# Zeros of the experts' results on ScalarE in place of GpSimd, a conversion moved, ten more constant products

## The chip, the cores and the metric

The kernel runs on one core of one Trainium2 chip. TensorE multiplies matrices into PSUM; VectorE, ScalarE and GpSimd work element by element; SP issues most transfers. The metric is device time in microseconds, the median of the runs.

## What is computed

The reference is clustered attention, a gated mixture of experts on its result, and a dense two-layer block behind that:

```python
mask = q_assign[:, :, :, None] == k_assign[:, :, None, :]       # nearest of 16 centroids
scores = np.where(mask, scale * np.matmul(q, k.transpose(0, 1, 3, 2)), -1e9)
attn = np.matmul(softmax(scores), v)                             # 2 x 8 heads, 768 x 64
x = attn.transpose(0, 2, 1, 3).reshape(1536, 512)
expert_idx = np.argmax(x @ w_gate, axis=1)                       # 8 experts
for e in range(E):                                               # each token by its expert
    out[mask_e] = gate_w[mask_e, None] * (np.maximum(xe @ w1[e], 0.0) @ w2[e])
h = out @ w_in                                                   # 512 -> 2048
return (np.maximum(h, 0.0) + alpha * np.minimum(h, 0.0)) @ w_out
```

## The kernel before

The instructions of each engine run in the order in which the program gives them; there is no scheduler, so that order is the one in which they stand in the code. Engines wait for each other by semaphores.

**Opening and attention.** Eight pairs of heads are worked on in turn. For the first pair the opening (from L658 on) assigns keys and queries to centroids in two halves: `sim_pair` (L345, products with the centroids), `simev_pair` (L352, ScalarE), `simturn_pair` (L358, transposes), `simmax_pair` and `simeq_pair` (L363, L369, VectorE), `eqt_pair` (L377), `eqev_pair` (L382, ScalarE), `first_pair` (L391 and L392 on TensorE, then L396 on ScalarE and L397 on VectorE). In between stand `qhi_pair` (L310) and `qlo_pair` (L314), which split queries in two parts, and copies on SP's queue. `warm(n, ps)` (L269 to L271) puts n products of constants in TensorE's queue, whose results nobody reads; they stand at places of the opening where TensorE waits for another engine. Then the loop over query tiles begins: `scores` (L429, L430), `rowmax` (L436, VectorE), `softmax` (L446, ScalarE), transposes (L460), and products with the values (L469).

**Experts.** Tokens are sorted by expert into DRAM (`Xs`, scatters by GpSimd at L612), and the experts run in order of their token counts, `blk` 0 to 7, each with eight groups: g = 8 * blk + f. At g, `l1` makes eight (for most experts) matmuls (L1004) into one of two PSUM banks, which ScalarE empties with a Relu (L1006); `l2` makes eight matmuls (L1025) for the group of g - 2. Expert 1 (`HB`) is computed in split parts: its weights are split by `wsplit` (L984 ScalarE, L985 VectorE) from g = 7 on, its matmuls are L989 to L991. Its tokens are transposed (`x_transp`, L963) at g = 5 and g = 6 in two halves, through two PSUM banks that ScalarE (L967) and VectorE (L968) empty. At the end of an expert `y_evac` (L1034, L1036) writes its result to the columns of `x2a` and `x2b` that belong to its tokens; the columns of overflowing tokens are not written there and must be zero. So `x2a` and `x2b`, 128 x 2 x 1842 floats each, are zeroed first: eight GpSimd memsets (L943) of 921 columns, which stand right before the experts. Their memory is that of rows and offsets that the last scatters read, and so is free only when these have landed.

**Conversions.** Among the experts stand 26 conversions of the dense block's weights from 64-bit to 32-bit floats (`CONV`, L1182: how many steps at which g). One `conv_step(k)` issues `conv_bits` (L178 to L181, four VectorE instructions) for k, the store of k - 1 on SP's queue (L234), `conv_abs` (L174, ScalarE) for k + 1, and for k of 6 and more the load of k + 3 on SP's queue. For k of 2 and more, up to 4, the next conversion's target is memory that this conversion reads, so its L174 waits for this one's L181. Four more, prefetched ones have L174 at g = 2, 4, 33, 37 and their four VectorE steps one group later, ahead of that group's `x_transp`. Weight blocks of the experts (1 MB each) are loaded on SP's queue as blocks come free (L147).

In a group the order of issue is: `l1`, `l2`, `y_evac`, the small sums of g (`side`), prefetched and split steps (`ahead`), transfers, `x_transp`, then the steps of `CONV`.

Of the kernel before, what the change touches and what calls it, by code (L numbers as in the profile page):

```python
# [14 lines left out]
AF = mybir.ActivationFunctionType  # L15
# [6 lines left out]
P = 128  # L22
# [16 lines left out]
XCOLS = N + CMAX  # L39
# [52 lines left out]
def tile_cluster_attention_moe(ctx: ExitStack, tc: tile.TileContext, qk, kk, v, cen, cenr, gate, mw, m2w,  # L92
                               alpha, consts, table, pos, zeros, nowhere, out):
    nc = tc.nc
# [11 lines left out]
    cst = const.tile([P, C_END], F32, name="cst")  # L106
# [156 lines left out]
    psS = [PS[:, 1024 * i:1024 * i + S] for i in range(2)]  # L263
# [5 lines left out]
    def warm(n, ps):  # L269
        for _ in range(n):  # L270
            nc.tensor.matmul(ps[:, 0:512], oneb, oneb.unsqueeze(1).broadcast_to([P, 4, P]), start=True, stop=True)  # L271
# [36 lines left out]
    def qhi_pair(p, hh, cs=slice(0, S)):  # L308
        st, R = sets[p % 2], Rt[p]
        nc.scalar.activation(st["QB"][0:64, hh, cs], R[0:64, hh, cs], AF.Copy, scale=0.125)  # L310
# [37 lines left out]
    def simev_pair(p, hh=None):  # L348
        pr = p % NPAIR
        rs, _, ps = alone(p, hh)  # L350
        sT = once("sT", p, [P, CH], tag="fr")
        nc.scalar.activation(sT[rs], ps[rs, :CH], AF.Copy, scale=cn[rs, 3, pr:pr + 1])  # L352
# [7 lines left out]
    def simmax_pair(p, hh=None):  # L360
        _, gs, ps = alone(p, hh)
        m = once("am", p, [P, 3, 8])
        nc.vector.tensor_reduce(m[:, :, gs], groups(ps[:, :CH])[:, :, gs], AX.X, ALU.max)  # L363

    def simeq_pair(p, hh=None):
        _, gs, ps = alone(p, hh)
        n = gs.stop - gs.start
        oh = once("ohc", p, [P, CH], BF16)
        nc.vector.tensor_tensor(groups(oh)[:, :, gs], groups(ps[:, :CH])[:, :, gs],  # L369
                                pre["am"][1][:, :, gs].unsqueeze(3).broadcast_to([P, 3, n, NC]), ALU.is_equal)  # L370
# [8 lines left out]
    def eqev_pair(p, hh=None):  # L379
        rs, _, ps = alone(p, hh)  # L380
        pb = ps.bitcast(BF16)
        nc.scalar.activation(once("eT", p, [P, CH], BF16)[rs], pb[rs, :CH], AF.Copy)  # L382

    def first_pair(p, hh=None):
        rs, _, ps = alone(p, hh)
        eT = pre["eT"][1]
        if hh is not None:

            st, r0 = sets[p % 2], rs.start
            pk = (psT, psM)[hh]  # L390
            nc.tensor.matmul(pk[r0:r0 + 48, :CH], firstb[rs, r0 + NC:r0 + NC + 48], eT[rs], start=True, stop=True)  # L391
            nc.tensor.matmul(ps[rs, :CH], firstb[rs, rs], eT[rs], start=True, stop=True)  # L392
            for c in range(2):
                cs = slice(c * CH, (c + 1) * CH)
                r1 = r0 + 32 * c
                nc.scalar.activation(st["QB"][64:80, hh, cs], ps[r1:r1 + 16, :CH], AF.Relu)  # L396
                nc.vector.tensor_scalar(st["KB"][64:80, hh, cs], pk[r1:r1 + 16, :CH], 0.0, -NEG, ALU.is_le, ALU.mult)  # L397
            return
        nc.tensor.matmul(psM[:, :CH], firstb, eT, start=True, stop=True)
# [82 lines left out]
    class Route:  # L482
# [101 lines left out]
        def sum(self):  # L584
            for k in range(self.n):
                nc.vector.tensor_add(ohsum, ohsum, OH[:, self.t0 + k, :])
                yield
# [67 lines left out]
    nc.vector.tensor_scalar_add(cn[:, 2, :], cn[:, 1, :], 1e-6)  # L655
    nc.vector.reciprocal(cn[:, 3, :], cn[:, 2, :])

    warm(8, psS[1])  # L658
    qhi_pair(0, 0)
    sim_pair(0, 0)  # L660
    simev_pair(0, 0)
    warm(2, psS[1])
    qhi_pair(0, 1)
    qlo_pair(0, 0)
    copyq_pair(0, h0)
# [1 line left out]
    nc.vector.tensor_copy(firstb, cst[:, C_FIRST:C_FIRST + P])  # L667
    simturn_pair(0, 0)
    simmax_pair(0, 0)
    warm(1, psS[1])  # L670
    simeq_pair(0, 0)
    ksplit_pair(0, nc.vector, 0)
    copy_pair(0, h0)
    load_r(1)
    eqt_pair(0, 0)
    eqev_pair(0, 0)
    warm(1, psS[1])
    first_pair(0, 0)
    qlo_pair(0, 1)
    sim_pair(0, 1)  # L680
# [193 lines left out]
    def parts(blk):  # L874
        return PARTS[blk], CAPS[blk] // PARTS[blk]
# [61 lines left out]
    x2p = pool(ctx, "x2p", side="right")  # L937
    x2a = x2p.tile([P, 2, XCOLS], F32, name="x2a")
    x2b = x2p.tile([P, 2, XCOLS], F32, name="x2b")
    for t in (x2a, x2b):  # L940
        for h in range(2):
            for c in range(0, XCOLS, XCOLS // 2):
                nc.gpsimd.memset(t[:, h, c:c + XCOLS // 2], 0.0)  # L943

    def x_transp(blk, half=None):
        nt, np_ = parts(blk)
        nb = nt * np_
        xr = xrt[blk]
        if half != 1:
            xts[blk] = xtp.tile([P, 4, CMAX], F32R if blk == HB else F32, name=f"x_{blk}", tag="x")[:, :, 0:nb]  # L950
            if blk == HB:
                split["x"] = xq.tile([P, 4 * CH], F32R, name="xlo", tag="x0")[:, 0:4 * nb].rearrange("p (d n) -> p d n", d=4)
                hlo = xq.tile([P, 4 * CH], F32R, name="hlo", tag="x1")
                split["h"] = [hlo[:, CMAX * i:CMAX * i + nb] for i in range(4)]
        x = xts[blk]
        dn = 2 if 2 * nb <= 512 else 1
        for g in range(4 // dn) if half is None else range(2 * half, 2 * half + 2):
            ps = bank(2 + g % 2)[:, 0:dn * nb]
            for k in range(dn):
                d = dn * g + k  # L960
                for t in range(nt):
                    c0 = k * nb + t * np_
                    nc.tensor.transpose(ps[:, c0:c0 + np_], xr[0:np_, t, d * P:(d + 1) * P], idf[0:np_, 0:np_])  # L963
            pv = ps.rearrange("p (d n) -> p d n", d=dn)
            if blk == HB:
                cs = slice(dn * g, dn * (g + 1))
                nc.scalar.activation(x[:, cs, :], pv, AF.Copy)  # L967
                nc.vector.tensor_sub(split["x"][:, cs, :], pv, x[:, cs, :].bitcast(F32))  # L968
            elif g % 2 == 0:
                nc.scalar.activation(x[:, dn * g:dn * (g + 1), :], pv, AF.Copy)  # L970
            else:
                nc.vector.tensor_copy(x[:, dn * g:dn * (g + 1), :], pv)
# [40 lines left out]
    def l2(blk, f):  # L1013
        nb = CAPS[blk]
        ci = 4 * blk + 2 * (f // 4) + 1
        w = wslots[ci].rearrange("p (f d) -> p f d", f=4)
        h = hts.pop((blk, f))
        if f == 0:
            yps[blk] = [bank(4 + o) for o in range(4)]
        for o in range(4):  # L1020
            y = yps[blk][o][:, 0:nb]
            if blk == HB:
                thrice(y, split[1, f], o, h, split["h"][f % 4], f == 0, f == 7)
            else:
                nc.tensor.matmul(y, w[:, f % 4, o * P:(o + 1) * P], h, start=f == 0, stop=f == 7)  # L1025
        if f % 4 == 3:
            wload()
# [134 lines left out]
    def s_half(r, n):  # L1162
# [10 lines left out]
        else:  # L1173
# [5 lines left out]
    NG = 8 * NB  # L1179


    CONV = {1: 1, 2: 1, 4: 1, 10: 1, 13: 1, 17: 1, 18: 1, 19: 1, 20: 1, 21: 1, 22: 1, 24: 1, 25: 1, 27: 1, 28: 1, 30: 1,  # L1182
            32: 1, 34: 1, 36: 1, 38: 1, 40: 1, 43: 1, 45: 1, 49: 1, 52: 1, 57: 1}
    assert sum(CONV.values()) == NCA
    xt = stmp.rearrange("p a d f -> p (a d f)")[:, 0:2 * CH].rearrange("p (a c) -> p a c", a=2)
# [86 lines left out]
    for g in range(NG + LAG):  # L1272
        if g < NG:
            blk, f = divmod(g, 8)
            l1(blk, f)
        if g >= LAG:
            b2, f2 = divmod(g - LAG, 8)
            l2(b2, f2)
            if f2 == 7 and b2 + 1 < NB:
                y_evac(b2, col[b2])  # L1280

        for f_ in side.get(g, []):
            f_()
        if g == 42:
            SHL = xsp.tile([P, 2, 7, 2, P], F32R, name="SHL", tag="SHL")
        for f_ in ahead.get(g, []):
            f_()
        if g == 40:
            more = nc.values_load(ovi[0:1, 0, 2:3], min_val=0, max_val=NSEL)
        if g < NG:  # L1290
            if f == 1 and blk + 1 < NB:
                wreg[blk + 1] = reg(wi[0:1, blk + 1:blk + 2], [ET.SP], 4 * (E - 1))
                row = reg(rowi[0:1, blk + 1:blk + 2], [ET.Activation if blk else ET.SP], E * N - N)
                x_load(blk + 1, Xs[ds(row, CAPS[blk + 1]), :])
            if f == 2:
                if blk >= 1:
                    src = offi[0:1, blk:blk + 1]
                    col[blk] = ds(reg(src, COMP, N), CAPS[blk])
                    put_places(blk, ds(reg(src, [ET.SP], N), CAPS[blk]))
                else:  # L1300
                    nc.sync.dma_start(PG[col[0], :], Xs[0:CAP, DM:XW])
            if f >= 5 and blk + 1 < NB and 2 * CAPS[blk + 1] > 512:
                if f < 7:
                    x_transp(blk + 1, f - 5)
            elif f == 6 and blk + 1 < NB:
                x_transp(blk + 1)
        if g == 0:
            conv_begin(0)
        for _ in range(CONV.get(g, 0)):
            conv_step(nconv[0])  # L1310
            nconv[0] += 1
# [186 lines left out]
    with tc.For_i(0, more, 1):  # L1498
# [27 lines left out]
        h = xo.tile([P, 2 * DM], F32, name="oh")  # L1526
# [16 lines left out]
        z = bank(5)  # L1543
# [78 lines left out]
```

## Time and profile before

| | us |
|---|---|
| median of three runs | 702.34 |
| lowest, highest | 701.82, 703.73 |
| the profiled execution | 704.18 |
| its span | 702.3 |
| TensorE matmul busy in it | 679.4 (97%) |
| VectorE busy | 482.2 (69%) |
| ScalarE busy | 370.8 (53%) |
| GpSimd busy | 68.8 (10%) |

The page gives the busy time of each engine, the chain of work that ended last and the costliest groups; the trace behind it gives single instructions with start and length, and the idle time of the engine before them with what ended it. PE is TensorE's matmuls, PEld its weight loads, DVE VectorE, ACT ScalarE, POOL GpSimd. The granted clock is a share of 2.4 GHz: 0.50 is 1.2 GHz. A row with x8 merges eight instructions in a row of one kind; its length runs from the first start to the last end.

### The profile page before, as it was taken

How to read it: one execution, taken by the hardware profiler on the slowest of the kernel's cores; microseconds unless marked ns; L12 is line 12 of the kernel's file. 1: busy time of each engine (PE TensorE's matmuls, PEld its weight loads, DVE VectorE, ACT ScalarE, POOL GpSimd, SP SyncE). 2: the span in 40 equal slices, each digit the busy share in tenths (PEclk: the TensorE clock that was granted, in tenths of full speed). 3: DMA queues.
4: the chain of work that ended last, by engine and by line, in shares of the span. 5: the costliest groups of instructions: out<-in, count | busy, mean ns of one | idle time of the engine just before them, and what ended most of it. 6: DMA issues, size and time to landing. Idle time of an engine off the chain costs nothing.

```text
span 702.3 us, 11396 instructions
## 1 busy us (share of the span) xinstructions
PE 679.4 (97%) x4126; PEld 574.4 (82%) x4126; DVE 482.2 (69%) x885; ACT 370.8 (53%) x735; POOL 68.8 (10%) x75
## 2 busy tenths in 40 slices
PE   7899999999999999799999999999999999999994
PEld 3667667666677689799999999989898998898983
DVE  6877777688886569587647654687788774544552
ACT  4877778767586512433323433664556654433441
POOL 3210202203120034000000000000000020000003
PEclk8999999999999999999999999999999999999997
DMA  8345887625246045386999989554433665554412
GB/s 261 107 159 157 272 297 257 204 79 169 76 103 217 27 151 196 98 279 149 396 337 314 353 311 297 147 201 154 157 135 136 203 199 170 162 157 143 149 32 92
DMA packets 49146, 131.78 MB, mean 188 GB/s; under 512 B 8399, under 2 KB 14054, under 8 KB 44896
## 3 DMA queue, kind: packets, MB, share of 16 engines
q1 hardware_dynamic: 44424, 115.85, 50.2%
q0 software_dynamic: 3216, 12.60, 5.3%
q10 hardware_dynamic: 1447, 2.58, 1.5%
q8 instruction: 34, 0.56, 0.3%
q14 instruction: 25, 0.20, 0.1%
HBM read 98.15 MB, written 30.24 MB: 183 GB/s over the span
## 4 chain that ended last, share of the span: by engine, by line
PE 86%; DVE 6%; issue 2%; DMA 2%; ACT 2%; POOL 1%; POOLq 0%; DVEq 0%; ACTq 0%; SPq 0%
PE PS L1226 16%; PE PS L1004 10%; PE PS L1025 10%; PE PS L460 8%; PE PS L469 8%; PE PS L1360 6%; PE PS L1359 6%; PE PS L1358 6%; PE PS L429 4%; PE PS L430 4%; DVE sm L436 2%; PE PS L989 1%; PE PS L990 1%; PE PS L991 1%; PE PS L345 1%
## 5 line engine op out<-in xcount | busy, mean ns | idle before, releaser
L446 ACT ACTIVATE P<-PS,sm 128x768 f32<-128x768 f32 x96 | 86.5, 901 | 32.0 <-DVE sm L436 32.0
L436 DVE TENSOR_REDUCE sm<-PS 128x1 f32<-128x768 f32 x96 | 91.9, 957 | 15.6 <-PE PS L430 15.2
L460 PEld LDWEIGHTS PS<-cst,P 128*128 128x128 f32 x576 | 63.4, 140 | 29.5 <-ACT P L446 17.3
L460 PE MATMUL PS<-cst,P 128*128 128x128 f32 x576 | 82.4, 278 | 3.2 <-ACT P L446 1.5
L1004 PE MATMUL PS<-x,w 128*128 128x208 f32 (+6 forms) x448 | 80.2, 323 | 0.0
L1025 PE MATMUL PS<-h,w 128*128 128x208 f32 (+6 forms) x448 | 79.7, 321 | 0.0
L463 DVE COPY PT<-PS 128x384 f32<-128x384 f32 x96 | 53.0, 552 | 37.9 <-PE PS L460 37.8
L1360 PE MATMUL PS<-BH,gc 128*128 128x512 f32 x192 | 75.8, 395 | 0.0
L1359 PE MATMUL PS<-BL,gc 128*128 128x512 f32 x192 | 75.5, 393 | 0.0
L1358 PE MATMUL PS<-BH,gc 128*128 128x512 f32 x192 | 75.1, 391 | 0.0
L429 PE MATMUL PS<-KA,QA 128*128 128x512 f32 x192 | 74.1, 386 | 0.0
L1004 PEld LDWEIGHTS PS<-x,w 128*128 128x128 f32 x448 | 72.3, 191 | 0.5 <-ACT h L1006 0.3
L1025 PEld LDWEIGHTS PS<-h,w 128*128 128x128 f32 x448 | 72.7, 191 | 0.1
L469 PE MATMUL PS<-PT,V 128*64 128x384 f32 (+1 forms) x432 | 72.4, 462 | 0.0
L1226 PE MATMUL PS<-xT,SHL 128*128 128x384 f32 x336 | 68.2, 338 | 0.2 <-DVE gc L1456 0.2
L1226 PEld LDWEIGHTS PS<-xT,SHL 128*128 128x128 f32 x336 | 59.6, 188 | 4.9 <-DVE gc L1456 0.7
L462 ACT ACTIVATE PT<-PS 128x384 f32<-128x384 f32 x96 | 46.7, 486 | 28.5 <-PE PS L460 26.9
L430 PE MATMUL PS<-KB,QB 96*128 96x512 f32 x192 | 61.4, 341 | 0.0
L1006 ACT ACTIVATE h<-PS 128x208 f32<-128x208 f32 (+7 forms) x64 | 21.3, 334 | 63.7 <-PE PS L1004 55.0
L1371 POOL DMA_INDIRECT out_dram<-row,PGR x12 | 11.7, 972 | 410.0 <-ACT row L1368 400.5
L1226 PE MATMUL PS<-xB,SHL 128*128 128x384 f32 x240 | 48.5, 337 | 0.0
L1226 PEld LDWEIGHTS PS<-xB,SHL 128*128 128x128 f32 x240 | 42.9, 188 | 3.1
(270 smaller groups left out, 1124.2 us busy)
## 6 DMA issues: line engine op xcount, KB each, us to landing
w<-in_mw SPq DMA_DIRECT2D x32, 1024.0 KB
SS<-SHL SPq DMA_DIRECT2D x24, 512.0 KB
SHL<-SS SPq DMA_DIRECT2D x24, 512.0 KB
raw<-in_m2w SPq DMA_DIRECT2D x20, 512.0 KB
bwr<-WB SPq DMA_DIRECT2D x16, 512.0 KB
R<-in_qk SPq DMA_DIRECT2D x7, 768.0 KB
KA<-in_kk POOLq DMA_DIRECT2D x7, 768.0 KB
Xs<-in_zeros SPq DMA_DIRECT2D x8, 614.4 KB
```

Source lines behind the costliest of these rows:

```text
L429: nc.tensor.matmul(ps[:, ks], st["QA"][:, hh, q0:q0 + P], st["KA"][:, hh, ks], start=True, stop=False)
L430: nc.tensor.matmul(ps[:, ks], st["QB"][0:96, hh, q0:q0 + P], st["KB"][0:96, hh, ks], start=False, stop=True)
L436: nc.vector.tensor_reduce(smt[s], psS[s % 2], AX.X, ALU.max, negate=True)
L446: nc.scalar.activation(Pt, psS[s % 2], AF.Exp, bias=smt.pop(s)[:, 0:1], accum_out=RS[:, tt, h:h + 1])
L460: nc.tensor.transpose(v4[:, kt // 3, kt % 3, :], Pt[:, kt * P:(kt + 1) * P], idf)
L469: nc.tensor.matmul(psO[64 * hh:64 * hh + 64, qs], V[:, kt, 64 * hh:64 * hh + 64], PTs[u][:, hh, kt, qs], start=kt == 0, stop=kt == KT - 1)
L1004: nc.tensor.matmul(ps, w[:, d, fs], x[:, d, :], start=d == 0, stop=d == 3)
L1025: nc.tensor.matmul(y, w[:, f % 4, o * P:(o + 1) * P], h, start=f == 0, stop=f == 7)
L1226: mm = lambda d, h, x, first, last: nc.tensor.matmul(ps, SHL[:, h, i, d, :], x[:, d, :], start=first and start, stop=last, skip_group_chec ...
L1358: nc.tensor.matmul(y, gh[n][:, i, c], whi, start=start, stop=False)
L1359: nc.tensor.matmul(y, gh[n][:, i, c], wlo, start=False, stop=False)
L1360: nc.tensor.matmul(y, gl[n][:, i, c], whi, start=False, stop=last)
```

## The change

Three edits. The eight memsets are taken out, and the same memory is written by twelve ScalarE instructions of 614 columns each: a copy, with scale zero, of one constant column that is broadcast. They are issued in groups g = 0 to 4, behind `x_transp` and ahead of the steps of `CONV`: three, three, two, two, two. The conversion step that stood at g = 4 (the third) moves to g = 10, and the list of the next two shifts with it: steps 2, 3, 4 stand at g = 10, 13, 16 in place of 4, 10, 13. And four calls of `warm` in the opening grow: 8 to 10, 2 to 5, 1 to 4, 1 to 3.

```diff
-    warm(8, psS[1])
+    warm(10, psS[1])
     qhi_pair(0, 0)
     sim_pair(0, 0)
     simev_pair(0, 0)
-    warm(2, psS[1])
+    warm(5, psS[1])
@@
     simmax_pair(0, 0)
-    warm(1, psS[1])
+    warm(4, psS[1])
@@
     eqev_pair(0, 0)
-    warm(1, psS[1])
+    warm(3, psS[1])
     first_pair(0, 0)
@@
-    for t in (x2a, x2b):
-        for h in range(2):
-            for c in range(0, XCOLS, XCOLS // 2):
-                nc.gpsimd.memset(t[:, h, c:c + XCOLS // 2], 0.0)
+    ZC = -(-XCOLS // 3)
+    zeros_ = iter([t[:, h, c:min(c + ZC, XCOLS)] for t in (x2a, x2b) for h in range(2) for c in range(0, XCOLS, ZC)])
+
+    def zero_x2(n):
+        for _ in range(n):
+            z = next(zeros_)
+            nc.scalar.activation(z, cst[:, 0:1].broadcast_to([P, z.shape[1]]), AF.Copy, scale=0.0)
@@
-    CONV = {1: 1, 2: 1, 4: 1, 10: 1, 13: 1, 17: 1, 18: 1, 19: 1, 20: 1, 21: 1, 22: 1, 24: 1, 25: 1, 27: 1, 28: 1, 30: 1,
+    CONV = {1: 1, 2: 1, 10: 1, 13: 1, 16: 1, 17: 1, 18: 1, 19: 1, 20: 1, 21: 1, 22: 1, 24: 1, 25: 1, 27: 1, 28: 1, 30: 1,
@@
+        if g < 5:
+            zero_x2(3 if g < 2 else 2)
         if g == 0:
             conv_begin(0)
```

## Rows read from the trace of the kernel before

**Rows 1.** The page's chain that ended last, by engine
```profile
PE 86%; DVE 6%; issue 2%; DMA 2%; ACT 2%; POOL 1%; POOLq 0%; DVEq 0%; ACTq 0%; SPq 0%
```

**Rows 2.** Busy time in stretches: us, busy per engine (count), granted clock, DMA
```profile
280.80:289.50 8.70, 5.04 (x22) 4.87 (x22) 5.51 (x11) 3.95 (x10) 0.00 (x0) 0.80 0.23 63
...
340.00:455.00 115.00, 114.96 (x770) 114.09 (x769) 71.71 (x127) 44.98 (x103) 0.00 (x0) 1.00 0.90 304
```

**Rows 3.** The same view, the opening
```profile
6.20:9.10 2.90, 1.37 (x9) 0.49 (x7) 2.63 (x12) 0.58 (x1) 0.00 (x0) 1.00 1.08 316
9.10:10.55 1.45, 1.03 (x4) 0.47 (x5) 0.92 (x1) 1.22 (x2) 0.87 (x1) 0.51 0.99 280
10.55:16.30 5.75, 5.73 (x18) 2.69 (x18) 3.63 (x6) 3.47 (x5) 4.27 (x4) 0.53 0.78 231
```

**Rows 4.** Instructions in order of time, the opening: start us, us, engine line
```profile
1.01 3.59 PE L271 MATMUL PS<-oneb 128*128 128x512 bf16 x8 [1.01 <-POOL oneb L631]
...
6.22 0.60 PE L271 MATMUL PS<-oneb 128*128 128x512 bf16 x2
...
7.15 0.58 ACT L352 ACTIVATE sT<-PS,cn 64x384 f32<-64x384 f32 x1 [1.19 <-DVE cn L656]
...
10.57 0.48 PE L391 MATMUL PS<-eT,firstb 64*48 64x384 bf16 x1 [0.44 <-ACT eT L382]
...
11.30 1.49 PE L345 MATMUL PS<-R,CB 128*32 128x384 f32 x4
...
12.77 0.99 PE L429 MATMUL PS<-KA,QA 128*128 128x512 f32 x1
...
14.65 0.96 DVE L436 TENSOR_REDUCE sm<-PS 128x1 f32<-128x768 f32 x1 [1.47 <-PE PS L430]
...
15.96 0.59 PE L429 MATMUL PS<-KA,QA 128*128 128x512 f32 x1
...
17.06 0.96 DVE L436 TENSOR_REDUCE sm<-PS 128x1 f32<-128x768 f32 x1 [0.79 <-PE PS L430]
```

**Rows 5.** The same view, GpSimd, start of the first expert
```profile
266.40 3.28 POOL L943 MEMSET x2a<- 128x921 f32 x4 [2.10 <-ACT h L1006]
269.62 3.84 POOL L943 MEMSET x2b<- 128x921 f32 x4
```

**Rows 6.** The same view, VectorE, first expert
```profile
266.89 3.06 DVE L178 TENSOR_SCALAR cv<-cv 128x512 f32<-128x512 f32 x1 [0.23 <-ACT cv L174]
...
278.63 0.42 DVE L178 TENSOR_SCALAR cv<-cv 128x512 f32<-128x512 f32 x1
...
280.89 0.55 DVE L178 TENSOR_SCALAR wA<-wA 128x768 f32<-128x768 f32 x1
...
283.94 0.85 DVE L968 TENSOR_TENSOR xlo<-PS,x 128x306 fp32r<-128x306 f32 x2
```

**Rows 7.** The same view, ScalarE, first expert
```profile
281.06 0.67 ACT L174 ACTIVATE wA<-wA 128x512 f32<-128x512 f32 x1 [4.38 <-DVE cv L181]
281.63 0.33 ACT L1006 ACTIVATE h<-PS 128x208 f32<-128x208 f32 x1
```

**Rows 8.** The same view, TensorE, first expert and start of the second
```profile
268.57 1.57 PE L1004 MATMUL PS<-x,w 128*128 128x208 f32 x8
...
284.46 0.86 PE L963 MATMUL PS<-cst,xr 102*128 102x102 f32 x6 [3.65 <-DVE xlo L968]
...
285.16 2.58 PE L1004 MATMUL PS<-x,w 128*128 128x208 f32 x8
...
289.53 0.45 PE L989 MATMUL PS<-x,wq 128*128 128x306 f32 x1
```

**Rows 9.** Groups by line and shape, ScalarE: count, busy us, mean ns
```profile
L984 ACT ACTIVATE wq<-w 128x512 fp32r<-128x512 f32 x9 | 5.3, 622 | 0.0
...
L1130 ACT ACTIVATE xB<-x2b 128x768 fp32r<-128x768 f32 x4 | 3.3, 834 | 0.0
```

**Rows 10.** Instructions in order of time, VectorE, start of the third expert
```profile
322.81 0.48 DVE L1036 COPY x2a<-PS 128x306 f32 x1 [3.68 <-PE PS L991]
```

## The prediction

> **What bounds the kernel now.** I read the chain of work that ended last first: TensorE holds 86% of it [rows 1], so what counts is where TensorE waits or runs at its lower clock. Stage by stage [rows 2], the stretch from 280.8 to 289.5 us stands out: 5.04 us of work in 8.7 us at a mean clock of 0.80, while from 340 to 455 us TensorE is busy for 114.96 of 115 us. The second such place is the opening: from 10.55 to 16.3 us the granted clock is 0.53, nearly all of it at 1.2 GHz [rows 3]. The change touches both places. In the rest of the kernel TensorE is the bound, and its loads and stores are released by its own progress, so time won at either place should last to the end.
>
> **Why TensorE stops at 280.8.** It waits 3.65 us, until 284.46, for a PSUM bank that VectorE empties (L968) [rows 8]. VectorE is late because its queue holds, in this order, conversions 0 and 1, the first prefetched conversion, conversion 2, the second prefetched conversion (280.89 to 283.94) and then L968 at 283.94 [rows 6]. Two things swell that queue. GpSimd's zeros run from 266.40 to 273.46 [rows 5], and the one L178 that starts beside them takes 3.06 us where the undisturbed one takes 0.42 [rows 6]: 2.64 us lost, and smaller losses on the two tensor_scalars that follow. And conversion 2 takes 2.26 us of the queue (278.63 to 280.89). ScalarE adds to it: its L174 at 281.06 had stood 4.38 us behind conversion 2, with the L1006 evacuation at 281.63 queued behind it [rows 7]. After the stop comes the clock: eight matmuls that take 1.57 us take 2.58 at 285.16 [rows 8].
>
> **Part 1, the zeros on ScalarE.** Eight GpSimd writes go and nothing else waits in GpSimd's queue there. Twelve ScalarE writes of 614 columns come (3, 3, 2, 2, 2 in groups g = 0 to 4). No row shows ScalarE with a broadcast column as input. The nearest are 0.622 us for 512 columns and 0.834 for 768 [rows 9]; between them 614 columns give 0.71. One instruction starts 0.10 us before the one ahead of it ends (0.67 long at 281.06, the next starts at 281.63 [rows 7]), so I count 0.60 a write, with 0.52 and 0.74 as ends from the two rows.
>
> What waits behind them: ScalarE's own L1006, which empties the bank that the next-but-one L1004 needs, and the first step (L174) of each conversion. The first write can't begin before the memory is free, which the start of the zeros shows: 266.40 [rows 5]; ScalarE stands until then. From there ScalarE runs, in us: three zeros 266.4 to 268.2, L174 of conversion 0 to 268.87, L1006 of g = 1 by 269.1, three zeros, L174 of conversion 1 by 271.5, L1006 of g = 2 by 271.7, the first prefetched L174 (0.9, estimated: the 0.67 for 512 columns [rows 7] and the 0.21 between the two widths of [rows 9]) and two zeros, L174 of conversion 2, L1006 of g = 3 by 274.5, two zeros, L1006 of g = 4 by 276.0, the second prefetched L174 to 276.8, two zeros, L1006 of g = 5 by 278.2.
>
> TensorE against that: a group of eight starts every 1.41 us (1.57 with its tail), and that of g = 3 starts at 268.57 [rows 8] with the one before it ending at 268.74. It now waits for the L1006 at 269.1: 0.4 us lost. At 271.97 (g = 4), 274.8 (g = 5) and 278.2 (g = 6) ScalarE is ahead. TensorE comes to the bank of L968 at 281.0.
>
> VectorE: conversion 0 from 268.9 (before: 266.89), 2.26 each without GpSimd beside it; conversion 1 from 271.5; the prefetched ones, 3.05 each (280.89 to 283.94 [rows 6]), to 276.9 and from 277.0 to 280.1; the first L968 ends by 280.6. That is 0.4 us before TensorE needs it, so the stop of 3.65 us goes, and the slow clock after it too. Late next is the hand-over into the second expert: L1006, weight split on ScalarE, then on VectorE, about 1.7 us after the last L1004, against 1.41 us of TensorE work: 0.3 us of waiting. The second expert's first L989, at 289.53 before [rows 8], comes at about 284.7: 4.8 us. I take 4.6, since 0.2 for hand-overs between engines is likely missing; ends from the write at 0.74 and 0.52 are 3.7 and 4.9 (below 0.65 a write VectorE no longer decides, above it ten writes stand before its last conversion).
>
> **Part 2, the third conversion moved.** Each step is four VectorE instructions, the store of the conversion before on SP, and L174 of the next, which waits for those four. The list shifts by one place: g = 4, 10, 13 become g = 10, 13, 16, so g = 10 and 13 hold as much as before and the addition falls at g = 16. There VectorE has stood idle for 3.68 us until 322.81 [rows 10]; 2.26 us and ScalarE's 0.67 fit. If the cover were gone, 2.9 us. On SP's queue the stores move behind weight loads that no longer wait for them, and no reader of the stored blocks runs before the last expert; SP's first store comes no later than before. Its gain is already in the queue above; on the path, nothing more.
>
> **Part 3, ten products.** Before: eight products in 3.59 us and two in 0.60 at 6.22 [rows 4] fit a step of 0.43 us at 1.2 GHz, half of that at 2.4, and one tail of 0.17; after the fall to 0.51 at 9.1 [rows 3] L429 takes 0.99 us, against 0.59 at 15.96 [rows 4]. Before the fall TensorE was busy for 1.37 of 2.9 us [rows 3]. Two more at the head end at 5.46 instead of 4.60; the first similarity behind them (1.49 at the lower clock, 11.30) ends by 7.0 at the latest, and its consumer, L352 on ScalarE, waits for VectorE until 7.15 [rows 4]. Three more behind it at 0.21 each fill 6.3 to 7.6, before L352 ends at 7.73; three more fill up to 9.1; two more up to 10.3, before L391, which waits for ScalarE until 10.57 [rows 4]. At 2.4 GHz none pushes real work by more than 0.1.
>
> If the clock then stays up, L391, L345, L429 and L430 run 0.6 times as long. VectorE's two waits for TensorE's scores, 1.47 us before 14.65 and 0.79 before 17.06 [rows 4], vanish: VectorE was free from 13.18 and takes up the first row maximum there, or 0.16 earlier, as L391 (0.48) ends earlier at full clock; L345 takes 0.9 in place of 1.49, and the scores, from about 12.1 and 0.6 long, are there by then. That is 2.2 us, carried into the attention loop, which runs on TensorE and these two engines with no load in its way. If the clock falls as before, the two extra products at 9.5 take 0.43 each and push L391: 0.3 lost. If it never rises before 9 us the twelve products there cost up to 2.0. I take 2.2, since six of the ten lie ahead of the fall and put 1.3 us of work on top of the 1.37.
>
> Here a rule of the Trainium skill weighs against me. The rows show a fall to 1.2 GHz near 9.1 us after a half-idle stretch, once, in one execution. The Trainium skill's page "TensorE: Matmul & The Clock Gate" (section on the HAM clock gate) says that the gate judges activity on a grid of its own that does not start with the kernel, so that the same kernel changes clock at different points from run to run. By it the ten products would be worth anything from nothing to 2.2 us in one run; this case has one trace before and can't show that.
>
> **The sum.** 4.6 + 2.2 = 6.8 us. The profiled execution took 704.18 us with a span of 702.3 and lies 1.84 above the median of the runs, 702.34. The same gain gives 697.4 for a profiled execution and 702.34 - 6.8 = 695.5 us for the median.
>
> **Rivals.** (A) The clock in the opening falls anyway: TensorE's real instructions there use few columns, and ten products may not be enough. Against it: the waits are nearly filled. 702.34 - 4.6 + 0.3 = 698.0; 23%. (B) ScalarE's writes are dearer: above 0.65 us each, ten of them stand before VectorE's last conversion, 1.0 us per 0.1. At 0.95 (a row of about 1,024 columns would cost that by the slope of [rows 9]) 3.0 us of 4.6 go: 698.5; 9%. (C) The slow L178 isn't GpSimd's doing, and the 2.64 us and the smaller losses, about 4.2 in all, stay: VectorE reaches L968 near 284 as before, 702.34 - 2.2 = 700.1; 5%. Against it: the later tensor_scalars, with GpSimd idle, take 0.42. (D) Won time is given back in the weight stream or at g = 16, with a price of up to the whole: 700 to 702.3; 6%. (E) Slower: ScalarE becomes the bound of the first expert. Its place is the queue in front of L1006 at g = 1 to 5; its price 10 x (write - 0.65); it eats both gains from 1.33 us a write and makes the kernel 0.3% slower from 1.54, for example 705 at 1.6. Against it: no ScalarE row of this width comes near; 3%.
>
> **How the numbers follow.** Forecast 54% (own range 694.2 to 696.8), A 23, B 9, C 5, D 6, E 3. Forecast, A and B hold 86%; so 694.0 to 699.2, which takes in the ends of the write's price and of the opening. A measurement can tell about 0.3%, 2.1 us: below 700.2 lie the forecast, A, B and part of C, 88%; D and the rest of C are "same", 8%; E and something unseen, 4%.
>
> **What would show it.** Right: no TensorE wait for L968 near 281, granted clock 1.0 from there on, L178 at 0.42, L1006 of g = 1 near 269 (all less the opening's gain), ScalarE writes near 0.7 each; the clock at 1.0 from 9 to 16 us, row maxima near 13.0 and 14.8; no new TensorE wait near g = 16. Wrong: a clock that falls in the opening, writes over 0.75, or a wait for L968 that stays.

## The result and the profile after

| | median, us | ratio to the kernel before (95% interval) |
|---|---|---|
| kernel before, in the same comparison | 704.88 (six runs) | |
| changed kernel | 697.42 (six runs, 696.21 to 702.79) | 0.99 (0.9851 to 0.9949) |
| the same again, later, beside 13 runs of before at 702.72 | 696.54 (eight runs, 695.19 to 702.02) | 0.9914 (0.9881 to 0.9946) |

The changed kernel is faster by about 1%: by 7.0 us by the first ratio (0.01 x 704.88 = 7.0) and by 6.0 by the second (0.0086 x 702.72). The forecast was a gain of 6.8 and 695.5 us. 697.42 lies in its range of 694.0 to 699.2, but above the 694.2 to 696.8 of the forecast's own case and nearer to the 698.0 of rival A; the second median, 696.54, lies inside. So the time alone does not tell the two apart, and the rows below have to. The medians of before are not alike, 702.34, 704.88 and 702.72, since single executions of most of these kernels can be 5 to 8 us longer than the median; e4_no_warm shows one such execution. For the sizes of single steps I therefore use the profiled pair: 704.18 before, 698.15 after, spans 702.3 and 696.3, a gain of 6.0 against the forecast 6.8.

Where the gain arises is read from a few starting times of the two traces, in us:

| | before | after | lead of after |
|---|---|---|---|
| first row maximum (L436) | 14.65 | 13.49 | 1.16 |
| second row maximum | 17.06 | 15.11 | 1.95 |
| first matmul of the first expert | 262.95 | 261.68 | 1.27 |
| first matmul of the second expert | 289.53 | 282.99 | 6.54 |
| first matmul of the third expert | 317.03 | 310.80 | 6.23 |
| end of the span | 702.3 | 696.3 | 6.0 |

Two places, as forecast: the opening (1.95, of which 1.27 reaches the experts) and the first expert (5.27, of which 0.31 is given back in the second). From L943 on, lines of the changed kernel stand three higher than in the kernel before.

After, busy time in stretches (us, busy of TensorE, its weight loads, VectorE, ScalarE, GpSimd with counts, granted clock, DMA share, GB/s), the stretches of [rows 3] and the two of [rows 2]:

```profile
6.20:9.10 2.90, 2.42 (x13) 0.88 (x11) 2.63 (x12) 1.31 (x2) 0.27 (x1) 1.00 1.12 324
9.10:10.55 1.45, 1.45 (x9) 0.52 (x8) 1.45 (x1) 0.48 (x1) 1.45 (x1) 1.00 0.96 220
10.55:16.30 5.75, 4.51 (x25) 2.54 (x24) 5.40 (x8) 4.50 (x8) 3.23 (x4) 1.00 1.03 294
279.50:283.00 3.50, 3.50 (x26) 3.46 (x24) 0.98 (x3) 1.75 (x5) 0.00 (x0) 1.00 0.46 164
340.00:455.00 115.00, 114.39 (x759) 112.25 (x758) 72.14 (x129) 46.62 (x104) 0.00 (x0) 1.00 0.88 298
```

The clock stays at 2.4 GHz through the opening, and from 279.5 us to the second expert TensorE is busy for 3.50 of 3.50 us at full clock, where it had stood and then run slowly [rows 2].

After, instructions in order of time (start, us, engine, line, operation, count, idle time before it and what ended it), the opening:

```profile
6.05 1.25 PE L271 MATMUL PS<-oneb 128*128 128x512 bf16 x5
...
8.11 1.04 PE L271 MATMUL PS<-oneb 128*128 128x512 bf16 x4
...
8.84 1.80 POOL L319 TENSOR_TENSOR KA<-R,KA 64x768 fp32r<-64x768 f32 x1 [6.22 <-DMA KA<-in_kk]
...
9.06 2.38 DVE L319 TENSOR_TENSOR KA<-R,KA 64x768 fp32r<-64x768 f32 x1
...
9.38 0.82 PE L271 MATMUL PS<-oneb 128*128 128x512 bf16 x3
10.13 0.34 PE L391 MATMUL PS<-eT,firstb 64*48 64x384 bf16 x1
10.56 0.84 PE L345 MATMUL PS<-R,CB 128*32 128x384 f32 x4
11.37 1.11 DVE L397 TENSOR_SCALAR KB<-PS 16x384 fp32r<-16x384 f32 x2
...
13.49 0.96 DVE L436 TENSOR_REDUCE sm<-PS 128x1 f32<-128x768 f32 x1
...
15.11 0.96 DVE L436 TENSOR_REDUCE sm<-PS 128x1 f32<-128x768 f32 x1
```

L345 takes 0.84 us in place of 1.49, and the waits of VectorE ahead of the row maxima are gone [rows 4]. New is VectorE's L319 of 2.38 us beside GpSimd's L319; it holds up L397 and so the first scores.

After, the first expert, ScalarE, VectorE and TensorE (answers to [rows 5 to 8]):

```profile
265.11 1.92 ACT L946 ACTIVATE x2a<-cst 128x614 f32<-128x614 f32 x3 [1.48 <-DMA Xs<-xrow,di]
...
267.61 0.43 DVE L178 TENSOR_SCALAR cv<-cv 128x512 f32<-128x512 f32 x1 [2.22 <-ACT cv L174]
...
267.86 1.67 PE L1007 MATMUL PS<-x,w 128*128 128x208 f32 x8 [0.40 <-ACT h L1009]
...
271.14 1.30 ACT L946 ACTIVATE x2b<-cst 128x614 f32<-128x614 f32 x2
...
278.58 0.85 DVE L971 TENSOR_TENSOR xlo<-PS,x 128x306 fp32r<-128x306 f32 x2
...
279.77 0.69 PE L966 MATMUL PS<-cst,xr 102*128 102x102 f32 x6
...
282.99 0.45 PE L992 MATMUL PS<-x,wq 128*128 128x306 f32 x1
283.27 0.30 PE L993 MATMUL PS<-xlo,wq 128*128 128x306 f32 x1
283.63 0.41 PE L994 MATMUL PS<-x,wq 128*128 128x306 f32 x1
```

The zeros take 0.61 to 0.65 us a write (0.61 from one start to the next, 1.30 / 2 = 0.65 by a row of two with its tail); L178 takes 0.43 us; the transposes at 279.77 wait for nothing, where they had stood 3.65 us [rows 8]. What is left is 0.40 us ahead of the fourth group.

### The profile page after: what moved, and what is told of

The parts are those of the page before. It is cut to its first block, busy times and chain, and to the rows that moved or that the text cites. A ratio compares the mean times of both kernels' runs of the same rounds, so it can differ in the third digit from the quotient of the medians.

```text
span 696.3 us, 11413 instructions
## 1 busy us (share of the span) xinstructions
PE 677.3 (97%) x4136; PEld 572.5 (82%) x4136; DVE 481.5 (69%) x885; ACT 377.7 (54%) x747; POOL 61.5 (9%) x67
## 4 chain that ended last, share of the span: by engine, by line
PE 56%; DMA 1%; ACT 1%; DVE 1%; issue 1%; POOL 0%; another core or an unknown queue 0%; POOLq 0%; ACTq 0%; DVEq 0%
PE PS L1229 16%; PE PS L1028 9%; PE PS L1007 9%; PE PS L1365 6%; PE PS L1364 6%; PE PS L1363 6%; DMA w<-in_mw 1%; PE PS L994 1%; PE PS L992 1%; PE PS L993 1%; PE PS L966 1%; POOL out_dram L1376 0%; ACT gc L1345 0%; DVE SHL L1134 0%; DVE gc L1348 0%
## 5 line engine op out<-in xcount | busy, mean ns | idle before, releaser
L436 DVE TENSOR_REDUCE sm<-PS 128x1 f32<-128x768 f32 x96 | 91.8, 957 | 13.2 <-PE PS L430 12.7
L469 PEld LDWEIGHTS PS<-PT,V 128*64 128x64 f32 x432 | 25.8, 136 | 23.8 <-issue 20.4
```

Source lines behind the costliest of these rows:

```text
L436: nc.vector.tensor_reduce(smt[s], psS[s % 2], AX.X, ALU.max, negate=True)
L469: nc.tensor.matmul(psO[64 * hh:64 * hh + 64, qs], V[:, kt, 64 * hh:64 * hh + 64], PTs[u][:, hh, kt, qs], start=kt == 0, stop=kt == KT - 1)
```

## Experiments

The theory is the forecast's: GpSimd's zeros and the third conversion make VectorE late for L968, and the products keep the clock. Its rivals were that the clock falls anyway (A), dearer writes (B), a slow L178 that is not GpSimd's doing (C), time given back (D) and ScalarE as the bound (E). First each part alone, and the whole without the products, twelve runs each beside 35 runs of the kernel before (median 702.81).

**e1_zeros**, the kernel before with the zeros' edit alone:

```diff
-                nc.gpsimd.memset(t[:, h, c:c + XCOLS // 2], 0.0)
+            nc.scalar.activation(z, cst[:, 0:1].broadcast_to([P, z.shape[1]]), AF.Copy, scale=0.0)
```

> The kernel before with the zeros on ScalarE alone; the third conversion stays at g = 4 and the products stay as they were. Theory (two causes of one late VectorE queue, each worth part of the stop): conversion 0 runs at 0.42 us for its first step, but conversion 2 still stands ahead of the second prefetched one, so TensorE still stops for L968, by about 1.8 us in place of 3.65, and the granted clock stays at 1.0 behind so short a stop; gain 3 us over the kernel before. Rival (the slow L178 is the whole cause): no stop, gain 5 us. Rival (GpSimd's writes don't slow VectorE): L178 stays near 3 us beside nothing, gain at most 0.5 us or a loss.

**e2_conv**, the moved conversion alone:

```diff
-    CONV = {1: 1, 2: 1, 4: 1, 10: 1, 13: 1, 17: 1,
+    CONV = {1: 1, 2: 1, 10: 1, 13: 1, 16: 1, 17: 1,
```

> The kernel before with the third conversion moved alone; the zeros stay on GpSimd. Theory: the first L178 still takes 3 us, VectorE reaches L968 2.3 us earlier, TensorE stops for about 1.4 us, no fall of the clock; gain 3.5 us. Rival (the move is the whole gain): no stop, 5 us. Rival (the moved step finds no cover at g = 16): a new TensorE wait of 2 to 3 us near the third expert.

**e3_warm**, the ten products alone:

```diff
-    warm(8, psS[1])
+    warm(10, psS[1])
@@
-    warm(2, psS[1])
+    warm(5, psS[1])
@@
-    warm(1, psS[1])
+    warm(4, psS[1])
@@
-    warm(1, psS[1])
+    warm(3, psS[1])
```

> The kernel before with the ten products alone. Theory: granted clock 1.0 from 9 to 16 us, row maxima 1.2 to 2.2 us earlier, 1.4 to 1.8 us of it left at the experts; gain 1.2 to 2 us, the stop at the first expert as before. Rival (the opening of the changed kernel was early because its loads landed early in that execution): clock as before or no difference beyond 0.3 us. Rival (a rule by which the gate's grid is set at random): gains that scatter between 0 and 2.2 us from run to run.

**e4_no_warm**, the changed kernel with these four calls as before:

```diff
-    warm(10, psS[1])
+    warm(8, psS[1])
@@
-    warm(5, psS[1])
+    warm(2, psS[1])
@@
-    warm(4, psS[1])
+    warm(1, psS[1])
@@
-    warm(3, psS[1])
+    warm(1, psS[1])
```

> The changed kernel without the ten products: zeros on ScalarE and the conversion moved. Theory: no stop for L968, the second expert starts 5 us earlier against the end of the attention than before, gain 4.5 to 5.3 us, and the opening as before with the clock at 0.5 from 9 to 16 us. Rival (the parts overlap): less than 4 us.

| | median, us | ratio (95% interval) | first expert in the profile, us |
|---|---|---|---|
| before | 702.81 | | 26.58 |
| e1_zeros | 700.43 | 0.9961 (0.9926 to 0.9996) | 23.32 |
| e2_conv | 701.14 | 0.9956 (0.9923 to 0.999) | 22.75 |
| e3_warm | 701.84 | 0.997 (0.9942 to 0.9998) | 27.79 |
| e4_no_warm | 698.72 | 0.9933 (0.9899 to 0.9968) | 21.45 |
| after | 697.42 | 0.99 (0.9851 to 0.9949) | 21.31 |

(The row of after is the first comparison above, with its own runs of before; its first expert and that of before are differences in the table of starting times.)

Each part gains alone, though each interval only just leaves out 1. By the ratios the gains are 2.7 us (e1_zeros, 3 expected), 3.1 (e2_conv, 3.5), 2.1 (e3_warm, 1.2 to 2) and 4.7 (e4_no_warm, 4.5 to 5.3). What the products add to the other two is not told by the time: 698.72 against 697.42, with intervals that overlap. In the first expert zeros and move are not added up: 3.3 and 3.8 us alone (26.58 less 23.32 and 22.75), 5.1 together (e4_no_warm). Each leaves TensorE's stop shorter, and with either one the slow clock after it goes (granted clock 1.00 from 280 to 290 us in both). e1_zeros, VectorE and TensorE in the first expert:

```profile
267.24 0.43 DVE L178 TENSOR_SCALAR cv<-cv 128x512 f32<-128x512 f32 x1 [2.40 <-ACT cv L174]
...
280.99 0.87 PE L966 MATMUL PS<-cst,xr 102*128 102x102 f32 x6 [1.43 <-DVE xlo L971]
```

e2_conv, the same lines:

```profile
266.48 3.17 DVE L178 TENSOR_SCALAR cv<-cv 128x512 f32<-128x512 f32 x1 [0.23 <-ACT cv L174]
...
281.89 0.86 PE L963 MATMUL PS<-cst,xr 102*128 102x102 f32 x6 [1.37 <-DVE xlo L968]
```

With the zeros on ScalarE the first L178 takes 0.43, with GpSimd's zeros in place 3.17: rival C falls. In both a stop of 1.4 us is left, and the other part takes it away. e3_warm shows how dear GpSimd's zeros can become; GpSimd, VectorE and TensorE in its first expert:

```profile
264.18 3.28 POOL L943 MEMSET x2a<- 128x921 f32 x4 [2.00 <-DMA Xs<-xrow,di]
267.40 3.28 POOL L943 MEMSET x2b<- 128x921 f32 x4
...
264.86 6.10 DVE L178 TENSOR_SCALAR cv<-cv 128x512 f32<-128x512 f32 x1 [0.23 <-ACT cv L174]
...
274.71 1.67 PE L1004 MATMUL PS<-x,w 128*128 128x208 f32 x8 [2.38 <-ACT h L1006]
...
283.93 1.28 PE L963 MATMUL PS<-cst,xr 102*128 102x102 f32 x6 [2.77 <-DVE xlo L968]
```

Here the one L178 stood until the last of the eight writes was done: 6.10 us, against 3.06 in the kernel before [rows 6]. This execution came to the experts 2.04 us earlier than before (260.91 against 262.95) and to the second expert only 0.83 earlier (288.70 against 289.53), and at the end nothing is left of it (span 702.5 against 702.3). It is the slowest of the twelve, 704.32 us: in the median 1.0 us is left, and the interval allows 0.1 to 4.1. So without the other two parts the products' gain can be lost in the first expert; that it always is, is not shown.

In the openings without the products the clock fell in all four executions, each at its own point: near 9.1 us before, 9.4 in e2_conv, 9.5 in e1_zeros and 7.6 in e4_no_warm. From 6.2 to 9.1, 9.1 to 10.55 and 10.55 to 16.3 us it was 1.00, 0.51 and 0.53 before [rows 3]. The stretches of e1_zeros:

```profile
9.10:10.55 1.45, 1.31 (x6) 0.52 (x6) 1.45 (x1) 0.48 (x1) 1.45 (x1) 0.64 0.95 229
10.55:16.30 5.75, 5.18 (x24) 2.74 (x24) 5.43 (x8) 4.30 (x7) 3.34 (x4) 0.79 1.03 295
```

And of e4_no_warm, where the fall came earlier:

```profile
6.20:9.10 2.90, 1.54 (x6) 0.49 (x4) 2.48 (x11) 1.00 (x2) 0.00 (x0) 0.75 0.82 254
9.10:10.55 1.45, 1.25 (x5) 0.62 (x6) 1.07 (x2) 0.90 (x2) 0.26 (x1) 0.50 0.76 155
10.55:16.30 5.75, 5.75 (x24) 2.92 (x22) 3.67 (x7) 3.68 (x6) 4.69 (x4) 0.66 1.03 239
```

What the products are worth thus depends on how long the clock would have been low: the second row maximum came at 17.06 before, 17.06 in e2_conv, 16.26 in e4_no_warm and 15.42 in e1_zeros, where the clock was back at 1.00 from 13 us on. With the products it came at 15.11 in after and at 15.39 in e11_after below, hardly earlier than in e1_zeros: in such a pair of executions they are worth next to nothing.

The profiled execution of e4_no_warm took 705.81 us, 7 more than its median. Its TensorE in the attention loop:

```profile
128.90 0.77 PE L429 MATMUL PS<-KA,QA 128*128 128x512 f32 x1 [3.90 <-DMA QA<-QB]
```

A copy that the next pair's scores need came late on SP's queue, and with the lower clock behind it (0.59 from 126 to 132 us, 0.88 from 132 to 140) its lead on the kernel before went from 0.8 to -5.7 us. In none of the other profiles does this copy hold TensorE, so I count it to none of the three edits.

**e5_zeros_twice**, the changed kernel with every zero piece written twice by ScalarE; the second write is work that the kernel does not need:

```diff
-            nc.scalar.activation(z, cst[:, 0:1].broadcast_to([P, z.shape[1]]), AF.Copy, scale=0.0)
+            for _ in range(2):
+                nc.scalar.activation(z, cst[:, 0:1].broadcast_to([P, z.shape[1]]), AF.Copy, scale=0.0)
```

> The changed kernel with each of the twelve zero pieces written twice by ScalarE, one right behind the other. In the changed kernel a write takes 0.61 to 0.65 us, ten of them stand ahead of the last prefetched conversion, and the first expert takes 21.31 us from its first matmul to the second expert's. If ScalarE's queue is what sets VectorE's conversions (rival E's mechanism: price 10 more writes), the stage grows by some 5 us (10 x 0.61 less about 1 us of slack on VectorE) to 26 to 27.5 us, TensorE waits for the evacuations of ScalarE in the groups after the zeros, and the run is 4 to 6 us longer than the changed kernel. If the writes lie beside TensorE's work with room to spare, the stage stays under 22.5 us.

One run, 702.22 us, 4.07 above the profiled run of after. Its first expert takes 28.62 us (259.48 to 288.10), 7.31 more than after. Its lead on before was 2.20 us larger than after's at the first expert, and from the second expert to the end it lost 1.0 less, so the run shows less than the stage. TensorE and ScalarE in the first expert (lines are one higher than in after):

```profile
263.09 4.16 ACT L947 ACTIVATE x2a<-cst 128x614 f32<-128x614 f32 x6 [1.66 <-DMA Xs<-xrow,di]
...
268.08 1.67 PE L1008 MATMUL PS<-x,w 128*128 128x208 f32 x8 [2.81 <-ACT h L1010]
...
272.91 1.68 PE L1008 MATMUL PS<-x,w 128*128 128x208 f32 x8 [1.75 <-ACT h L1010]
...
277.22 1.67 PE L1008 MATMUL PS<-x,w 128*128 128x208 f32 x8 [1.23 <-ACT h L1010]
...
284.71 0.87 PE L967 MATMUL PS<-cst,xr 102*128 102x102 f32 x6 [1.05 <-DVE xlo L972]
```

The mechanism of rivals B and E is real: ScalarE's queue has no room for a second set. It is paid mostly at ScalarE's evacuations (2.81, 1.75, 1.23) and less at the transposes behind VectorE (1.05), and with 28.62 us the stage is dearer than the 26 to 27.5 expected: a write of these pairs takes 0.69 us (4.16 / 6, with its tail) where it took 0.64 in after (1.92 / 3), and both kinds of wait are paid. Rival E's price fits: with 0.68 from one start to the next a piece costs 1.36, and 10 x (1.36 - 0.65) is 7.1 of the 7.31. At the 0.61 to 0.65 us that a write takes, the change pays little of it.

**e6_pool_gate**, the changed kernel with GpSimd's split in the opening held behind VectorE's:

```diff
+    after0 = ep.tile([P, 1], F32, name="after0")
+    nc.gpsimd.tensor_copy(after0[64:128], sets[0]["KA"].bitcast(F32)[64:128, 0, 0:1])
     ksplit_pair(0, nc.gpsimd, 1)
```

> The changed kernel, with one GpSimd copy of a single column put ahead of GpSimd's split of the second half in the opening; it reads what VectorE's split of the first half writes, so that the two splits no longer run side by side. If GpSimd's split is what makes VectorE's take 2.38 us in place of 0.95, VectorE's takes 0.95 again, the threshold step behind it starts at about 10.7 in place of 11.37, and the first two row maxima come at 12.9 to 13.1 and 14.5 to 14.7 in place of 13.49 and 15.11. If VectorE's split is slow for another reason (its input arriving late), both row maxima stay where they are.

One run, 696.34 us. Its opening, GpSimd and VectorE:

```profile
9.07 0.95 DVE L319 TENSOR_TENSOR KA<-R,KA 64x768 fp32r<-64x768 f32 x1
...
10.41 1.81 POOL L319 TENSOR_TENSOR KA<-R,KA 64x768 fp32r<-64x768 f32 x1
...
11.65 1.38 DVE L314 SCALAR_TENSOR_TENSOR QA<-R,QB 64x768 fp32r<-64x768 f32 x1
13.06 0.96 DVE L436 TENSOR_REDUCE sm<-PS 128x1 f32<-128x768 f32 x1
```

VectorE's split takes 0.95 again and the first row maximum comes at 13.06, the second at 14.60, as expected. But now VectorE's L314 runs beside GpSimd and takes 1.38 in place of 0.95. That the order of starts decides is shown by executions without the gate. In e5_zeros_twice GpSimd's split started after VectorE's, and the row maxima came at 12.63 and 14.25:

```profile
9.07 0.95 DVE L319 TENSOR_TENSOR KA<-R,KA 64x768 fp32r<-64x768 f32 x1
9.53 2.16 POOL L319 TENSOR_TENSOR KA<-R,KA 64x768 fp32r<-64x768 f32 x1 [6.92 <-DMA KA<-in_kk]
```

In after it started at 8.84, ahead of VectorE's at 9.06, and in e1_zeros, whose opening is that of the kernel before, the same happened:

```profile
8.94 1.80 POOL L319 TENSOR_TENSOR KA<-R,KA 64x768 fp32r<-64x768 f32 x1 [6.33 <-DMA KA<-in_kk]
9.07 2.49 DVE L319 TENSOR_TENSOR KA<-R,KA 64x768 fp32r<-64x768 f32 x1
```

The start hangs on a load's landing, which is not the same from one execution to the next; it is not a product of the change.

**e7_zeros_g1**, the changed kernel with the zeros one group later:

```diff
-        if g < 5:
-            zero_x2(3 if g < 2 else 2)
+        if 1 <= g < 5:
+            zero_x2(3)
```

> The changed kernel with the zeros at groups 1 to 4, three each, in place of 3, 3, 2, 2, 2 at groups 0 to 4. If the first zero's wait for the last scatter (1.48 us) and the three writes behind it are what makes the evacuation of group 1 late, that evacuation no longer stands behind them, the 0.4 us wait of TensorE ahead of group 3 goes, the first conversion starts 2 us earlier, and the first expert takes 20.8 to 21.0 us in place of 21.31. If the evacuation of group 2 becomes the late one instead, a wait of 0.3 to 0.6 stands ahead of group 4 and nothing is gained.

One run, 695.55 us; first expert 20.69 us (259.77 to 280.46), and no wait of TensorE in it:

```profile
263.44 1.92 ACT L946 ACTIVATE x2a<-cst 128x614 f32<-128x614 f32 x3 [0.31 <-DMA Xs<-xrow,di]
...
265.40 1.57 PE L1007 MATMUL PS<-x,w 128*128 128x208 f32 x8
```

So the 0.40 us was the evacuation behind the first three writes, and these behind the last scatter. The length of that wait is not the same in each execution: with the zeros written once and from group 0 on, TensorE stood ahead of the fourth group in all seven profiles (0.40 in after, 0.52 to 0.87 in e1_zeros, e4_no_warm, e6_pool_gate, e9_warm_head, e10_warm_tail and e11_after), with the zeros from group 1 on in none of three (this one, e8_both, e12_zeros_g1).

**e8_both**, the edits of e6_pool_gate and e7_zeros_g1 together:

```diff
+    nc.gpsimd.tensor_copy(after0[64:128], sets[0]["KA"].bitcast(F32)[64:128, 0, 0:1])
@@
+        if 1 <= g < 5:
+            zero_x2(3)
```

> The two edits together: GpSimd's split held back in the opening and the zeros at groups 1 to 4. If both work and add, 0.5 us in the opening and 0.4 in the first expert: 0.8 to 0.9 us below the changed kernel, a ratio to the kernel before of 0.988 to 0.990 against 0.99 for the changed kernel; too little for the time alone to tell, so the row maxima and the first expert's length have to show it. If time won early is given back at waits on loads, the span differs from the changed kernel's by less than 0.4.

Median 695.44 (695.02 to 696.10, six runs), ratio 0.9867 (0.9818 to 0.9916) beside ten runs of before with median 703.41. Its first expert is 20.70 us, its row maxima come at 13.28 and 14.82; L314 takes 1.38 as in e6_pool_gate, so the gate is no gain where GpSimd comes late by itself: without it, e7_zeros_g1 had 12.85 and 14.42. The first expert is 0.61 us shorter than after's, where 0.4 was expected; the 0.5 us expected in the opening did not come: its first row maximum is 0.21 ahead of after's and 0.43 behind that of e7_zeros_g1.

**e9_warm_head** and **e10_warm_tail**, the changed kernel with five of the ten products each:

```diff
-    warm(4, psS[1])
+    warm(1, psS[1])
@@
-    warm(3, psS[1])
+    warm(1, psS[1])
```

> The changed kernel with only the first two calls raised (10 and 5 products, the later two stay at 1): five of the ten products, all ahead of 7.6 us. The forecast's step says that the work put ahead of the fall near 9 us is what keeps the clock: then the granted clock stays 1.00 from 6 to 16 us and the row maxima come at 12.6 to 13.5 and 14.2 to 15.2. If each half-idle stretch has to be filled, the clock falls between 8 and 11 us and the row maxima come at 13.6 to 14.7 and 15.4 to 17.1, as in the kernels without the products.

```diff
-    warm(10, psS[1])
+    warm(8, psS[1])
@@
-    warm(5, psS[1])
+    warm(2, psS[1])
```

> The changed kernel with only the later two calls raised (4 and 3 products; the first two stay at 8 and 2): five of the ten products, between 8 and 10.3 us. By the forecast's step the stretch ahead of 9 us stays as half idle as before but for three products near 8.3 us, and the clock falls near 9 to 10 us: row maxima at 13.6 to 14.7 and 15.4 to 17.1. If what counts is the stretch from 8 to 10.5 us alone, the clock stays 1.00 and the row maxima come at 12.6 to 13.5 and 14.2 to 15.2.

One run each, 697.76 and 696.28 us. The granted clock was 1.00 from 6.6 to 16.3 us in both; row maxima 13.53 and 15.14 in e9_warm_head, where GpSimd's split again started ahead of VectorE's (8.87 against 9.06, VectorE's took 2.43), and 13.37 and 14.98 in e10_warm_tail, where VectorE's split waited until 9.44 for its load. For e10_warm_tail the fall was expected and did not come. It is no clean test of the forecast's reason, work ahead of the fall: TensorE was busy for 2.31 us of the 2.9 from 6.2 to 9.1 us, not half idle as before (1.37), since L345 ran at the lower clock until 6.66 and three of the five products lie ahead of 9.15. So either half was enough in the one execution seen of each; where the products have to stand, and that five of them hold the clock always, is not shown.

**e11_after** and **e12_zeros_g1**, the changed kernel and the kernel of e7_zeros_g1 side by side:

> The changed kernel itself, again, beside the next one on the same chip: 0.988 to 0.993 of the kernel before; its first expert 21.2 to 21.5 us, clock 1.00 through the opening, first row maximum at 12.6 to 13.5 (the later one where GpSimd's split starts ahead of VectorE's).

> The zeros at groups 1 to 4, three each, timed. One profile of it had the first expert at 20.69 us against 21.31. If that 0.6 us lasts to the end, its median is 0.3 to 0.9 us below the changed kernel's, too little for the interval to part the two, and both lie 6 to 8 us below the kernel before. If the scatter's landing varies from run to run, the wait at the zeros can also show only in some of the changed kernel's runs, and the medians lie within 0.3.

Medians 696.54 (eight runs, 695.19 to 702.02) and 696.08 (six runs, 694.97 to 697.36), ratios 0.9914 (0.9881 to 0.9946) and 0.9897 (0.9864 to 0.9929). The profiles have a wait of 0.61 us ahead of the fourth group in e11_after and none in e12_zeros_g1, with first experts of 21.53 and 20.70 us. The profiles part the two by 0.8 us, the medians differ by 0.46, and the intervals overlap: the later zeros are the better place by the trace, and by the time not told apart. The first row maximum of e11_after came at 13.78, later than the 12.6 to 13.5 expected, since GpSimd's split started at 9.12 and VectorE's, at 9.30, took 2.43.

## Why the prediction was right

**The price of a write** was forecast at 0.60 us and measured at 0.61 to 0.65. The wait for the scatter's landing ahead of the first one came (1.48 us), and the 0.4 us of TensorE at group 3 is the 0.40 of the trace. That this agrees so closely is luck, with 0.40 to 0.87 in the seven executions that have it; the mechanism is the forecast's (e7_zeros_g1).

**L178 and the stop.** L178 at 0.42 was forecast, 0.43 came. The first L971 started at 278.58 and TensorE came at 279.77, with no wait: the stop of 3.65 us and the slow clock behind it are gone.

**The hand-over** into the second expert was forecast as 0.3 us ahead of its first matmul. It stands behind the first two instead (283.27 to 283.63, some 0.2 us), and in the second expert, which is 0.31 longer. Both experts together took 54.08 us before and 49.12 after: 4.96 against the forecast 4.6. The 0.2 that I had kept for hand-overs between engines was not needed.

**The moved conversion** made no new wait near g = 16. Its own worth in the first expert was larger than the forecast let one see: 3.8 us alone, since it took away part of the stop and all of the slow clock by itself.

**The opening** was the term of the sum that was mis-sized: 2.2 forecast, 1.95 at the second row maximum and 1.8 up to 105 us in the attention (1.67 and 1.5 in e11_after). The clock did what was forecast; once at 2.4 GHz it stayed there through the opening in all ten profiled executions with five or ten more products, and it fell in all four without. The moment of its first rise, which differs between executions, does not part the two groups: 3.7 to 6.9 us in the ten, 4.2 to 6.1 in the four. The forecast had VectorE free at 13.0 and missed that GpSimd's split can start ahead of VectorE's L319 so that this takes 2.38 us. Where it did not (e3_warm, e5_zeros_twice, e7_zeros_g1, e12_zeros_g1), the lead was 2.4 to 2.7 us up to 105 us; where it did (after, e9_warm_head, e11_after), 1.5 to 1.8. So 2.2 is met by neither kind of execution: against this trace of before the clock is worth more than forecast, and the meeting takes 0.9 of it. And e1_zeros, without products and with the meeting, still had a lead of 1.65, since its clock was low for a shorter time: the term is not one number. A second meeting of the two engines cost after 0.45 of its lead near 108 us: GpSimd's L319 started at 106.43, and VectorE's L314 at 108.22 took 2.22 us. In the kernel before the load landed at the same time (GpSimd's L319 at 106.36), and VectorE, later by then, started its L314 at 110.01, when GpSimd was done; it took 0.54. In e11_after L314 took 1.74 there, and no lead was lost.

**The rivals.** A did not come. The Trainium skill's rule that spoke for it ("TensorE: Matmul & The Clock Gate", the section on the HAM clock gate) agrees with the traces in that the fall came at different points in the four kernels without the products, whose openings are the same code. C fell by e1_zeros and e2_conv. B and E have the right mechanism (e5_zeros_twice), but the write is too short for them. D is seen in small: a weight load (w<-in_mw) holds TensorE for 0.32 us at 433.06 in after, and not in e11_after. Added up: 1.27 at the first expert, 4.96 in the two experts, less 0.23 lost from the third on, is the 6.0 of the spans. That is 0.8 under the forecast: 0.93 less from the opening, 0.36 more from the experts, 0.23 given back.

## What to carry to other kernels

Look at each engine's slowest instruction of a form that is fast elsewhere (3.06 against 0.42 us): the engine beside it, not the instruction, can be the cost, and moving that other work is the thing to try. Price what moves by the queue that it joins: here twelve writes fitted into ScalarE and twelve more did not. Parts that remove the same stop do not add up, and a lead won early can be lost where a later stage meets a transfer, or another engine's work, that comes at a fixed time (0.45 us near 108 us here).

## What the runs showed of the hardware

A VectorE L178 that meets GpSimd's back-to-back writes is not held for one of them but for several: it took 3.06 us before and 3.17 in e2_conv, until the four writes to `x2a` were done, and 6.10 in e3_warm, until all eight were, each write being about 0.82 us (3.28 for four). L180 and L181, which have two inputs, took 0.69 us beside the same writes (271.08 and 271.81 before), as without them (279.55). The Trainium skill's page "SBUF — State Buffer" (section "Who interferes with whom") says that whichever of the two starts first has the shared ports for its whole instruction, and that the order of issue decides who is blocked. The order of starts agrees with L319 here (8.84 ahead of 9.06: VectorE 2.38 us; 9.07 ahead of 9.53: GpSimd 2.16). By the page, taken for each instruction by itself, L178 would be held for the one write that it met, 0.82 us at most; the 6.10 us differ, and the measurement decides.

The clock's fall in the opening came in all four executions without added products, at a point of its own in each (7.6 to 9.5 us), and in none of the ten with five or ten products that nobody reads.
